# Block 0 of a fused attention and GEGLU block: weight parts issued from another queue, outputs taken out in steps, VectorE in written order

## The chip, the cores and the metric

The kernel runs on one core of a Trainium2 chip. Its time is the device time of one execution in microseconds (us); of several runs the median is given. Engines are named as in the profile: PE (TensorE, matrix products), ACT (ScalarE), DVE (VectorE), POOL (GpSimd) and SP (SyncE, which here only issues DMAs). PSUM is the memory that PE writes into, in banks of 512 floats by 128 partitions; SBUF is the working memory of all engines.

## What is computed

One transformer block in float32 on x of 2048 x 512, with 32 heads of 16 columns that share one key and one value head:

```
q = LN(x) @ wq    k = LN(x) @ wk    v = LN(x) @ wv
p = softmax(q k^T / 4)  per head
h = x + (p v) @ wo
out = h + (gelu(LN(h) @ w_gate) * (LN(h) @ w_up)) @ w_down      # F = 1792
```

## The kernel before, in words

Rows of x are cut into four blocks of 512. A prologue normalizes x, forms the keys and values of all rows and the queries of block 0. Then the attention of blocks 0 to 3 runs, each in eight groups of four heads, and beside it the dense part (`wo`, the gate, up and down products) of the block before; the dense part of block 3 is a tail. float32 products are formed from a high and a low part of each operand, which `split` makes; so `wo` and the FFN weights have to be parted once.

For a group and a chunk of 128 keys, `score` (L614) is called twice. Each call (`scores`, L276) computes two heads' scores, on PE, into a tile `s` of two PSUM banks (three such tiles in block 0), and ACT writes the exponential to `p`. When both calls of a chunk are done, the chunk is put into the list `pend`; `finish` (L593) takes the oldest chunks out and `weigh` (L289) forms the products with the values, 16 matmuls for two chunks, into the one bank `acc`. After 16 chunks `evacuate` (L298) copies `acc` to `oT` on DVE, dumps it to DRAM (`acc_d`), loads it back turned into `oc` (four DMAs), and, after each second group, takes the reciprocal of the row sums in four pieces, multiplies, and splits the result into `o_hi` and `o_lo`.

Block 0 has a loop of its own (L649 to L671), with n counting the score calls: eight groups of 32 calls, and 16 more calls of block 1, up to `lead`. Four calls are called a period here. Beside the scores it carries:

- a step of `work` (the generator `later_q`, L221, over `project_q`, L163) in each period but one of eight: the queries of blocks 1 to 3. Such a step is mostly three matmuls into the single bank `pq`; after each four of them DVE splits the bank, and SP stores the pieces. After the 16 matmul steps of a block come the norms: `pn`, DVE's maximum `q2`, four small POOL operations on `mm` (L201 to L208), and DVE's `m` (L212).
- a step of `parts` (`part_weights`, L328) in most periods: 46 parts, 4 of `wo` and then, for each of 14 FFN columns f, the gate, up and down weights. A step stores the part before (42 stores in all, none for `wo`), loads the next raw weights, and parts the present ones on POOL (two operations, three for the down weights). `w_raw` and `w_both` have two buffers.
- `finish(2)` at a period's end.

PE, ACT and POOL work in the order in which the program is written (`manual_schedule`, L128); in this loop SP does so too (L642), while DVE's instructions are put in order by a scheduler. An engine waits at an instruction until what it needs is there, and everything behind it waits as well. A DMA stands in the queue of the engine that issues it. Semaphore waits between engines are set by the framework.

At n = 256 the rest of the parts is written, the early tiles are released, and the tiles of the dense part take their place; so the first loads of dense tiles (three `w`, L397) wait for the last store of a part. At n = 272 the planned chunks begin (L687), in which dense work is mixed in by written shares; their first dense product is `pp`, which reads `o_hi` and `o_lo` of block 0. `check_bound` (L950) writes a bound of the scores to DRAM and loads it back, and `bound_flag` (L957) makes a flag of it, which decides after everything else whether a second, exact way is taken; it is not taken with these inputs.

Of the kernel before, what the change touches and what calls it, by code (L numbers as in the profile page):

```python
# [9 lines left out]
F32 = mybir.dt.float32  # L10
F32R = mybir.dt.float32r
# [3 lines left out]
ALU = mybir.AluOpType  # L15
# [4 lines left out]
P = 128  # L20
# [16 lines left out]
def kernel(  # L37
# [62 lines left out]
    def split(eng_hi, hi, lo, src, eng_lo=None):  # L100
        if eng_hi is nc.scalar:
            nc.scalar.activation(hi, src, AF.Copy)
        else:
            eng_hi.tensor_copy(hi, src)  # L104
        (eng_lo or nc.vector).tensor_tensor(lo, src, hi.bitcast(F32), op=ALU.subtract)  # L105
# [28 lines left out]
    def run(outer, first):  # L134
# [28 lines left out]
        def project_q(b, eng):  # L163
            tsl = slice(b * T, (b + 1) * T)
            xT_hi, xT_lo = xT[b]
            qss = []
            for c in range(DC):
                pq = psum1(f"pq_{b}_{c}")
                n = 0
                for d in range(DC):  # L170
                    for wt, xt in ((wq_hi, xT_hi), (wq_hi, xT_lo), (wq_lo, xT_hi)):
                        nc.tensor.matmul(  # L172
                            pq, wt[:, d, c * P : (c + 1) * P], xt[:, d, :],
                            start=(n == 0), stop=(n == 3 * DC - 1),
                        )
                        n += 1
                    yield 3
                qh = eb.tile([P, T], F32R, tag="qh", bufs=2, name=f"qh_{b}_{c}")
                ql = eb.tile([P, T], F32R, tag="ql", bufs=2, name=f"ql_{b}_{c}")
                split(eng, qh, ql, pq)  # L180
                qs = eb.tile([P, T], BF16, tag="qs", bufs=DC, name=f"qs_{b}_{c}")
                (nc.vector if b else nc.gpsimd).tensor_tensor(
                    qs, qh.bitcast(F32), qh.bitcast(F32), op=ALU.mult
                )
                qss.append(qs)
                for r0, part in ((0, qh), (DH, ql), (2 * DH, qh)):
                    nc.sync.dma_start(
                        q_d[c * HC : (c + 1) * HC, r0 : r0 + DH, tsl].bitcast(F32),
                        part.bitcast(F32),
                    )  # L190
            yield 3
            pn = psum1(f"pqn_{b}")[:H, :]
            for c in range(DC):
                nc.tensor.matmul(pn, sel[:, c, :], qss[c], start=(c == 0), stop=(c == DC - 1))
            qn = eb.tile([H, T], F32, tag="qn", bufs=1, name=f"qn_{b}")
            nc.vector.tensor_copy(qn, pn)
            nc.vector.tensor_reduce(q2[:, b : b + 1], qn, axis=AX.X, op=ALU.max)
            yield 2

            mm = eb.tile([H, 3], F32, tag="mm", bufs=2, name=f"mm_{b}")  # L200
            nc.gpsimd.tensor_scalar(  # L201
                mm[:, 0:1], q2[:, b : b + 1], k2m, 1e-30, op0=ALU.mult, op1=ALU.add
            )
            nc.gpsimd.tensor_tensor(mm[:, 1:2], mm[:, 0:1], power[:H, 0:1], op=ALU.pow)
            nc.gpsimd.tensor_scalar(
                mm[:, 2:3], mm[:, 0:1], mm[:, 1:2], 0.5, op0=ALU.mult, op1=ALU.mult
            )
            nc.gpsimd.tensor_scalar(  # L208
                mm[:, 1:2], mm[:, 1:2], k2m, 0.5, op0=ALU.mult, op1=ALU.mult
            )  # L210
            m = eb.tile([H, T], F32R, tag="m", bufs=2, name=f"m_{b}")
            nc.vector.tensor_scalar(m, qn, mm[:, 1:2], mm[:, 2:3], op0=ALU.mult, op1=ALU.add)  # L212
            ms[b] = m
            if b > 0:
                nc.sync.dma_start(q_d[:, 3 * DH, tsl].bitcast(F32), m.bitcast(F32))
            yield 2
# [54 lines left out]
            nc.scalar.dma_start(q_d[:, 3 * DH, :T].bitcast(F32), m.bitcast(F32))  # L271
            return qg

        o_blk, pair = {}, [None]

        def scores(i, p, qg, kc, u):  # L276

# [17 lines left out]

        def evacuate(b, g, acc):  # L298
            oT = sb.tile([P, T], F32, tag="oT", bufs=2, name=f"oT_{b}_{g}")
            nc.vector.tensor_copy(oT, acc)  # L300
            nc.sync.dma_start(acc_d[:, g % 4, :], oT)
            c, k = divmod(g, 2)
            if k == 0:
                pair[0] = sb.tile([P, 2, T], F32, tag="oc", bufs=2, name=f"oc_{b}_{c}")
            oc = pair[0]
            view = acc_d[:, g % 4, :].rearrange("(j s e) t -> j e s t", s=2, e=DH)
            for j in range(4):
                r0 = 64 * k + DH * j
                nc.sync.dma_start(oc[r0 : r0 + DH, :, :], view[j])
            if k == 0:  # L310
                return
            if c == 0:
                o_blk[b] = [
                    sb.tile([P, DC, T], F32R, tag=f"o_{w}", bufs=1, name=f"o_{w}_{b}")
                    for w in ("hi", "lo")
                ]
            hi, lo = o_blk[b]

            for t in range(TB):
                sl = slice(t * P, (t + 1) * P)  # L320
                nc.vector.reciprocal(oc[:, 1, sl], oc[:, 1, sl])  # L321
            nc.vector.tensor_tensor(oc[:, 0, :], oc[:, 0, :], oc[:, 1, :], op=ALU.mult)
            split(nc.vector, hi[:, c, :], lo[:, c, :], oc[:, 0, :])

        late = ExitStack()
        db = None
# [1 line left out]
        def part_weights(pw):  # L328
# [4 lines left out]

            def load_wo(c):
                raw = pw.tile([P, D], F32, tag="w_raw", bufs=2, name=f"wo_raw_{c}")
                nc.sync.dma_start(raw, wo_t[:, c, :])
                return raw

            def part_wo(c, raw):
# [1 line left out]

            def load_f(src, name):
                raw = pw.tile([P, D], F32, tag="w_raw", bufs=2, name=f"{name}r")
                nc.sync.dma_start(raw.rearrange("p (c n) -> p c n", n=src.shape[-1]), src)
                return raw

            def part_f(name, halve, raw):
# [4 lines left out]
                return both  # L352

            def store_1(f, k, both):
                nc.sync.dma_start(
                    w1_d[f, :, :, k].bitcast(F32),
                    both.rearrange("p i (c n) -> p i c n", c=DC).bitcast(F32),
                )

            def store_2(f, both):  # L360
                nc.sync.dma_start(w2_d[f].bitcast(F32), both.bitcast(F32))

            steps = [
                (partial(load_wo, c), partial(part_wo, c), None) for c in range(DC)
# [228 lines left out]
        def finish(n):  # L593
            for _ in range(min(n, len(pend))):
                pb, pg, pkc, pp, pacc, _ = pend.pop(0)
                weigh(pacc, pp, pkc)
                if pkc == KC - 1:
                    evacuate(pb, pg, pacc)
# [40 lines left out]

        LEAD = (3, 2, 2)  # L640
        n, lead = 0, 2 * PER + sum(SIZES[: LEAD[0]])
        with tc.manual_schedule(engines={mybir.EngineType.SP}):  # L642
            parts = None
            if first:
                work = later_q()
                parts = part_weights(early.enter_context(tc.tile_pool(name="parts", bufs=1)))


            while n < lead:  # L649
                if n == 2 * PER:  # L650
                    drain()
                    for _ in parts or ():
                        pass
                    parts = None
                    early.close()
                    db = late.enter_context(tc.tile_pool(name="dense", bufs=1))

                if n % 4 == 3 and work is not None and n % (2 * KC) != 11:
                    if next(work, None) is None:
                        work = None  # L660
                score(n)
                n += 1
                if n % 4:
                    continue
                if len(pend) > 2:
                    finish(2)
                if parts is not None and n > 12 and n % 24:
                    next(parts, None)
                if n == 2 * PER + 4:
                    primed = dense(0)  # L670
                    next(primed)  # L671
        if first:
            bound_flag()
        work = primed
        set_banks("ps_rest")
        width = 3
# [10 lines left out]
        for c in range(LEAD[0], (NB - 1) * NG * len(SIZES)):  # L687
# [36 lines left out]
                work = None  # L724
            finish(sum(e[5] < n - 1 for e in pend) if cg < len(SIZES) - 1 else len(pend))
        drain()
        banks.close()
        held_banks.close()
        set_banks("ps_tail")
# [220 lines left out]
    def check_bound(sb, k2m):  # L950
        q2m = sb.tile([H, 1], F32, name="q2m")
        nc.vector.tensor_reduce(q2m, q2, axis=AX.X, op=ALU.max)
        nc.vector.tensor_tensor(q2m, q2m, k2m, op=ALU.mult)
        nc.sync.dma_start(b_d.rearrange("o h -> h o"), q2m)
        nc.sync.dma_start(b2, b_d)

    def bound_flag():  # L957
        nc.vector.tensor_reduce(b1, b2, axis=AX.X, op=ALU.max)

        nc.vector.tensor_scalar(flag, b1, (BOUND_MAX / SCALE) ** 2, None, op0=ALU.is_le)  # L960
# [69 lines left out]
```

## Time and profile before

| | |
|---|---|
| three runs | 1493.0, 1494.29, 1496.1 us; median 1494.29 |
| the profiled execution | 1492.66 us, of which the span of the trace is 1490.9 |
| mean granted PE clock | 0.988 |
| busy in the span | PE 1419.6 us (95%), ACT 1036.6 (70%), DVE 530.4 (36%), POOL 160.9 (11%) |
| DMA | 180.53 MB, 121 GB/s in the mean |

The page cuts the span into 40 slices of 37.3 us and gives each engine's busy share of a slice in tenths. A row of a timeline is: start and duration in us, engine, line, operation, output<-input, shapes, and in brackets how long the engine had been idle before it and who released it. `SPq` and `POOLq` are rows of DMA issues. The granted clock of PE stands in the windows' rows and on the page as a share of full speed.

### The profile page before, as it was taken

How to read it: one execution, taken by the hardware profiler on the slowest of the kernel's cores; microseconds unless marked ns; L12 is line 12 of the kernel's file. 1: busy time of each engine (PE TensorE's matmuls, PEld its weight loads, DVE VectorE, ACT ScalarE, POOL GpSimd, SP SyncE). 2: the span in 40 equal slices, each digit the busy share in tenths (PEclk: the TensorE clock that was granted, in tenths of full speed). 3: DMA queues.
4: the chain of work that ended last, by engine and by line, in shares of the span. 5: the costliest groups of instructions: out<-in, count | busy, mean ns of one | idle time of the engine just before them, and what ended most of it. 6: DMA issues, size and time to landing. Idle time of an engine off the chain costs nothing.

```text
span 1490.9 us, 24774 instructions
## 1 busy us (share of the span) xinstructions
PE 1419.6 (95%) x10412; PEld 755.2 (51%) x10412; DVE 530.4 (36%) x915; ACT 1036.6 (70%) x1139; POOL 160.9 (11%) x211
## 2 busy tenths in 40 slices
PE   6899999979999999999999999999999999997998
PEld 4533333324455555555455555554455555555886
DVE  7311221203342332423342423423342423425665
ACT  6499999977777777777777777777777777760000
POOL 5424445430000000000000000000000000000000
PEclk9899999999999999999999999999999999998999
DMA  4426776664132323222233223232233224232552
GB/s 160 154 72 197 234 222 216 215 202 151 57 111 78 115 82 118 103 85 97 68 111 110 87 79 138 76 121 69 68 111 110 89 76 138 72 106 79 189 193 85
DMA packets 76109, 180.53 MB, mean 121 GB/s; under 512 B 8506, under 2 KB 22842, under 8 KB 68790
## 3 DMA queue, kind: packets, MB, share of 16 engines
q1 hardware_dynamic: 75870, 178.81, 35.9%
q8 instruction: 83, 1.36, 0.4%
q14 instruction: 36, 0.29, 0.1%
q10 hardware_dynamic: 120, 0.07, 0.0%
HBM read 131.13 MB, written 47.71 MB: 120 GB/s over the span
## 4 chain that ended last, share of the span: by engine, by line
PE 64%; ACT 15%; DMA 6%; issue 5%; POOL 5%; DVE 2%; SPq 1%; ACTq 0%; POOLq 0%; DVEq 0%
PE acc L291 26%; ACT p L287 14%; PE s L283 13%; PE pu L412 5%; PE pd L412 4%; PE pg L412 4%; DMA w_1r<-in_B_w_up_dram 3%; PE pg L429 3%; PE pd L429 3%; PE pu L429 3%; DMA acc_d<-oT 2%; PE pp L412 1%; PE pq L172 1%; POOL w_1b L105 1%; PE pp L429 1%
## 5 line engine op out<-in xcount | busy, mean ns | idle before, releaser
L287 ACT ACTIVATE p<-s 128x1024 f32<-128x1024 f32 x1024 | 970.8, 1031 | 282.2 <-PE s L283 281.5
L291 PE MATMUL acc<-p,v_sb 128*32 128x512 f32 x4096 | 493.3, 600 | 4.9 <-DVE oT L300 4.9
L283 PE MATMUL s<-qg,kaug 50*128 50x512 f32 x1984 | 393.2, 434 | 29.9 <-ACT p L287 26.8
L283 PEld LDWEIGHTS s<-qg,kaug 50*128 50x128 f32 x1984 | 172.5, 184 | 311.8 <-ACT p L287 196.4
L291 PEld LDWEIGHTS acc<-p,v_sb 128*32 128x32 f32 x4096 | 112.5, 109 | 253.1 <-issue 237.7
L412 PE MATMUL pg<-x2h,w 64*128 64x512 f32 x672 | 232.0, 391 | 0.8 <-DVE x2h L104 0.8
L412 PE MATMUL pu<-x2h,w 64*128 64x512 f32 x672 | 232.1, 392 | 0.6 <-DVE x2l L105 0.6
L412 PE MATMUL pg<-x2l,w 64*128 64x512 f32 x336 | 131.9, 393 | 0.1
L412 PEld LDWEIGHTS pu<-x2h,w 64*128 64x128 f32 x672 | 124.7, 186 | 14.1 <-issue 1.4
L412 PE MATMUL pu<-x2l,w 64*128 64x512 f32 x336 | 131.6, 392 | 0.0
L412 PEld LDWEIGHTS pg<-x2h,w 64*128 64x128 f32 x672 | 124.7, 186 | 12.3 <-DVE x2h L104 2.0
L113 POOL TENSOR_SCALAR rstd<-mv 128x1 f32<-128x1 f32 x16 | 3.5, 219 | 1025.9 <-DVE mv L111 1025.9
L412 PE MATMUL pd<-w,gh 64*128 64x512 f32 x672 | 105.4, 391 | 0.3 <-DVE mark_pd L420 0.3
L526 ACT ACTIVATE ga<-ga 128x512 f32<-128x512 f32 x56 | 36.2, 646 | 91.4 <-DVE ga L521 91.4
L518 DVE COPY g<-pg 128x512 f32<-128x512 f32 x56 | 38.7, 691 | 143.1 <-PE pg L412 134.9
L554 DVE TENSOR_TENSOR h<-h,pd 128x512 f32<-128x512 f32 x64 | 41.9, 685 | 112.3 <-PE pd L412 91.3
L412 PEld LDWEIGHTS pd<-w,gh 64*128 64x128 f32 x672 | 63.3, 185 | 15.6 <-issue 0.8
L321 DVE RECIPROCAL oc<-oc 128x128 f32<-128x128 f32 x64 | 54.2, 908 | 43.7 <-DMA oc<-acc_d 43.7
L412 PE MATMUL pd<-w,gl 64*128 64x512 f32 x336 | 66.4, 392 | 0.0
L412 PEld LDWEIGHTS pg<-x2l,w 64*128 64x128 f32 x336 | 62.3, 185 | 8.0 <-DVE x2l L105 1.1
L412 PEld LDWEIGHTS pu<-x2l,w 64*128 64x128 f32 x336 | 62.3, 185 | 7.3
L527 DVE SCALAR_TENSOR_TENSOR ga<-ga,g 128x512 f32<-128x512 f32 x56 | 38.8, 692 | 69.8 <-ACT ga L526 69.8
(176 smaller groups left out, 1216.5 us busy)
## 6 DMA issues: line engine op xcount, KB each, us to landing
w<-w_d SPq DMA_DIRECT2D x84, 1024.0 KB
qg<-q_d SPq DMA_DIRECT2D x62, 200.0 KB
q_d<-qh SPq DMA_DIRECT2D x32, 256.0 KB
acc_d<-oT SPq DMA_DIRECT2D x32, 256.0 KB
oc<-acc_d SPq DMA_DIRECT2D x128, 64.0 KB
w_d<-w_0b SPq DMA_DIRECT2D x14, 512.0 KB
w_d<-w_1b SPq DMA_DIRECT2D x14, 512.0 KB
x<-in_A_x_dram SPq DMA_DIRECT2D x16, 256.0 KB
```

The lines of the kernel that those rows point to most:

```text
L105: (eng_lo or nc.vector).tensor_tensor(lo, src, hi.bitcast(F32), op=ALU.subtract)
L172: nc.tensor.matmul(pq, wt[:, d, c * P : (c + 1) * P], xt[:, d, :], start=(n == 0), stop=(n == 3 * DC - 1),)
L283: nc.tensor.matmul(s[:, a, :], kaug[rows, kc * P : (kc + 1) * P], qg[rows, u, :], start=True, stop=True,)
L287: nc.scalar.activation(p[:, 2 * u : 2 * u + 2, :], s, AF.Exp, scale=SCALE)
L291: nc.tensor.matmul(acc[32 * j : 32 * j + 32, :], v_sb[:, kc, :], p[:, j, :], start=(kc == 0), stop=(kc == KC - 1), skip_group_check=True,)
L321: nc.vector.reciprocal(oc[:, 1, sl], oc[:, 1, sl])
L412: nc.tensor.matmul(banks[k], lhsT[rows], rhs[rows], start=(turn == 0 and i == 0), stop=(turn == 1 and i == n - 1), skip_group_check=True,)
L429: nc.tensor.matmul(bank, lhsT, rhs, start=(i == 0), stop=(i == len(ts) - 1))
L518: nc.vector.tensor_copy(g, pg)
L526: nc.scalar.activation(a, a, AF.Tanh, scale=GELU_A * GELU_C)
L527: nc.vector.scalar_tensor_tensor(a, a, 1.0, g, op0=ALU.add, op1=ALU.mult)
L554: nc.vector.tensor_tensor(hs[t], hs[t], pd, op=ALU.add)
```

## The change

- The DMAs of `part_weights` (loads of raw weights and stores of the parts) are issued by GpSimd instead of SP.
- `evacuate` no longer issues everything at once. It makes `oT` and its dump, and puts what follows into a list `outs`: the four loads of `oc` (`turn_out`); after each second group also an empty step, two steps of two reciprocals, and the step `divide`. `take_out` takes one step out in each period. From block 1 on, and at the last group of block 0, all steps are taken at once.
- DVE, too, follows the written order in this loop.
- A step without work (`yield 0`) is put between `mm` and `m`.
- Whether a period gets a step of `work` is settled at its start (`given`; n % 32 is not 8). In a period without one, one chunk is weighed in the middle and one at the end.
- The load of the bound and the flag move behind block 3's attention; the load is issued by GpSimd.

```diff
@@ project_q
             m = eb.tile([H, T], F32R, tag="m", bufs=2, name=f"m_{b}")
+            yield 0
             nc.vector.tensor_scalar(m, qn, mm[:, 1:2], mm[:, 2:3], op0=ALU.mult, op1=ALU.add)
@@ evacuate
+        def take_out():
+            for step in outs.pop(0):
+                step()
...
-            view = acc_d[:, g % 4, :].rearrange("(j s e) t -> j e s t", s=2, e=DH)
-            for j in range(4):
-                r0 = 64 * k + DH * j
-                nc.sync.dma_start(oc[r0 : r0 + DH, :, :], view[j])
-            if k == 0:
-                return
...
+            def turn_out():
+                view = acc_d[:, g % 4, :].rearrange("(j s e) t -> j e s t", s=2, e=DH)
+                for j in range(4):
+                    r0 = 64 * k + DH * j
+                    nc.sync.dma_start(oc[r0 : r0 + DH, :, :], view[j])
...
+            def invert(t):
                 sl = slice(t * P, (t + 1) * P)
                 nc.vector.reciprocal(oc[:, 1, sl], oc[:, 1, sl])
...
+            outs.append([turn_out])
+            if k == 1:
+                outs.append([])
+                outs.extend([partial(invert, t), partial(invert, t + 1)] for t in (0, 2))
+                outs.append([divide])
+
+            if b > 0 or g == NG - 1:
+                while outs:
+                    take_out()
@@ part_weights: load_wo, load_f, store_1, store_2
-                nc.sync.dma_start(raw, wo_t[:, c, :])
+                nc.gpsimd.dma_start(raw, wo_t[:, c, :])
...
-                nc.sync.dma_start(w2_d[f].bitcast(F32), both.bitcast(F32))
+                nc.gpsimd.dma_start(w2_d[f].bitcast(F32), both.bitcast(F32))
@@ run
-        with tc.manual_schedule(engines={mybir.EngineType.SP}):
+        with tc.manual_schedule(engines={mybir.EngineType.SP, mybir.EngineType.DVE}):
...
-                if n % 4 == 3 and work is not None and n % (2 * KC) != 11:
-                    if next(work, None) is None:
-                        work = None
+                if n % 4 == 0:
+                    given = work is not None and n % (2 * KC) != 8
+                if n % 4 == 3 and given and next(work, None) is None:
+                    work = None
                 score(n)
                 n += 1
+                if n % 4 == 2 and not given and len(pend) > 2:
+                    finish(1)
                 if n % 4:
                     continue
                 if len(pend) > 2:
-                    finish(2)
+                    finish(len(pend) - 2)
+                if outs:
+                    take_out()
...
-        if first:
-            bound_flag()
+        assert not outs
...
         drain()
+        if first:
+            bound_flag()
@@ check_bound, bound_flag
-        nc.sync.dma_start(b2, b_d)
...
     def bound_flag():
+        nc.gpsimd.dma_start(b2, b_d)
         nc.vector.tensor_reduce(b1, b2, axis=AX.X, op=ALU.max)
```

More of the change, by code (lines that the diff above doesn't have):

```diff
@@ L272, in first_q @@
             return qg
-        o_blk, pair = {}, [None]
+        o_blk, pair, outs = {}, [None], []
         def scores(i, p, qg, kc, u):
@@ L305, in evacuate, with divide @@
             oc = pair[0]
-            view = acc_d[:, g % 4, :].rearrange("(j s e) t -> j e s t", s=2, e=DH)
-            for j in range(4):
-                r0 = 64 * k + DH * j
-                nc.sync.dma_start(oc[r0 : r0 + DH, :, :], view[j])
-            if k == 0:
-                return
[L312 to L319, printed above, removed]
+            def turn_out():
[4 more added lines that the diff above has]
+            def invert(t):
                 sl = slice(t * P, (t + 1) * P)
                 nc.vector.reciprocal(oc[:, 1, sl], oc[:, 1, sl])
-            nc.vector.tensor_tensor(oc[:, 0, :], oc[:, 0, :], oc[:, 1, :], op=ALU.mult)
-            split(nc.vector, hi[:, c, :], lo[:, c, :], oc[:, 0, :])
+            def divide():
+                if c == 0:
+                    o_blk[b] = [
+                        sb.tile([P, DC, T], F32R, tag=f"o_{w}", bufs=1, name=f"o_{w}_{b}")
+                        for w in ("hi", "lo")
+                    ]
+                hi, lo = o_blk[b]
+                nc.vector.tensor_tensor(oc[:, 0, :], oc[:, 0, :], oc[:, 1, :], op=ALU.mult)
+                split(nc.vector, hi[:, c, :], lo[:, c, :], oc[:, 0, :])
+            outs.append([turn_out])
[6 more added lines that the diff above has]
+                    take_out()
         late = ExitStack()
@@ L343, in load_f @@
                 raw = pw.tile([P, D], F32, tag="w_raw", bufs=2, name=f"{name}r")
-                nc.sync.dma_start(raw.rearrange("p (c n) -> p c n", n=src.shape[-1]), src)
+                nc.gpsimd.dma_start(raw.rearrange("p (c n) -> p c n", n=src.shape[-1]), src)
                 return raw
@@ L354, in store_1 @@
             def store_1(f, k, both):
-                nc.sync.dma_start(
+                nc.gpsimd.dma_start(
                     w1_d[f, :, :, k].bitcast(F32),
```

## The prediction, made before the changed kernel ran

> **What bounds the kernel now.** I read the page first, then ScalarE's timeline over block 0, then the same stretch on all engines where that timeline shows a hole, then SP's and GpSimd's own rows.
>
> ```profile
> span 1490.9 us, 24774 instructions
> PE   6899999979999999999999999999999999997998
> L287 ACT ACTIVATE p<-s 128x1024 f32<-128x1024 f32 x1024 | 970.8, 1031 | 282.2 <-PE s L283 281.5
> POOL rstd L113 <- DVE mv L111: 1025.9, 13, 315.6
> ```
>
> PE is full nearly everywhere except slice 9, about 298 to 335 us; GpSimd has no large work after its weight parts (its longest wait lies behind block 0). So block 0 (66 to 349 us) is the only place where this change can act: the instruction orders of PE and ScalarE from the first dense chunk on are the same in both kernels, and VectorE's differs there only by the two tiny flag operations. The forecast is the change of the moment at which PE reaches the first `pp`.
>
> A period of block 0 is four `score` calls: four exponentials on ScalarE, 16 weighing matmuls and, where a step of projection is given, three more matmuls.
>
> ```profile
> 92.19 3.77 ACT L287 ACTIVATE p<-s 128x1024 f32<-128x1024 f32 x4 [0.33 <-PE s L283]
> 96.27 3.77 ACT L287 ACTIVATE p<-s 128x1024 f32<-128x1024 f32 x4 [0.30 <-PE s L283]
> 299.21 3.77 ACT L287 ACTIVATE p<-s 128x1024 f32<-128x1024 f32 x4 [0.20 <-PE s L283]
> 310.14 3.77 ACT L287 ACTIVATE p<-s 128x1024 f32<-128x1024 f32 x4 [7.16 <-PE s L283]
> 314.10 3.77 ACT L287 ACTIVATE p<-s 128x1024 f32<-128x1024 f32 x4 [0.19 <-PE s L283]
> 291.25 3.77 ACT L287 ACTIVATE p<-s 128x1024 f32<-128x1024 f32 x4 [0.81 <-PE s L283]
> ```
>
> With projection the period is 96.27 - 92.19 = 4.08 us, without it 314.10 - 310.14 = 3.96. One exponential lasts 1.03 and four in a row 3.77, so the next starts 0.913 after the last: 3.67 would be ScalarE's own pace. One hole stands out: 299.21 to 310.14 is 10.93, that is 6.97 over 3.96.
>
> ```profile
> 301.47 1.26 POOL L105 TENSOR_TENSOR w212b<-w212r,w212b 128x512 fp32r<-128x512 f32 x1
> 302.84 0.26 POOL L201 TENSOR_SCALAR mm<-q,k2m 32x1 f32<-32x1 f32 x1
> 304.48 0.53 DVE L212 TENSOR_SCALAR m<-qn,mm 32x512 fp32r<-32x512 f32 x1 [14.22 <-POOL mm L208]
> 304.94 0.67 DVE L300 COPY oT<-acc 128x512 f32<-128x512 f32 x1
> 305.67 3.64 PE L291 MATMUL acc<-p,v_sb 128*32 128x512 f32 x16 [4.89 <-DVE oT L300]
> 311.65 0.64 PE L291 MATMUL acc<-p,v_sb 128*32 128x512 f32 x4
> ```
>
> This is the hole, read upward. PE waits 4.89 for `oT`, since `acc` has one buffer; then its 16 matmuls take 3.64 instead of 1.85 (315.61 below), the clock being lower after the rest. `oT` stood in VectorE's queue behind `m`, which waited 14.22 for GpSimd's `mm`, behind weight part 212.
>
> **The change, part by part.**
>
> (1) *VectorE in program order, and the extra yield.* The seventh `oT` now precedes the last `m`, and `m` comes one given period after its `mm`. The 6.97 go, as does the 0.81 - 0.20 = 0.6 at 291.25 (VectorE then worked through reciprocals and a split that had waited for one transfer). What is late next: the eighth `oT` stands behind that same `m`, eight periods later. I count -7.6.
>
> (2) *Weighing in the middle of a period without projection.* There are 15 such periods: one of eight in each of groups 1 to 7, four in group 8 (n = 232, 244, 248, 252), and four of the lead. PE's work in one is small enough:
>
> ```profile
> 315.18 0.50 PE L283 MATMUL s<-qg,kaug 50*128 50x512 f32 x2 [0.71 <-ACT p L287]
> 315.61 1.92 PE L291 MATMUL acc<-p,v_sb 128*32 128x512 f32 x16
> 317.47 0.96 PE L283 MATMUL s<-qg,kaug 50*128 50x512 f32 x6
> ```
>
> 16 weighing matmuls take 317.47 - 315.61 = 1.86, a pair of scores 0.43 (315.61 - 315.18), four pairs 1.72: 3.58 per period, under ScalarE's 3.67. Now they come in halves of 0.93 while ScalarE still holds up to three finished score tiles, so its gap of 0.19 to 0.30 closes: 15 x (3.96 - 3.69) = -4.0. Bounds: nothing, and 15 x (3.96 - 3.67) = -4.4.
>
> (3) *Outputs in steps.* The reciprocals follow `oT` after two periods (7.4 to 8.2 us). In the row of the last group, whose dump did not queue behind weight transfers, the data were there 344.15 - 337.43 = 6.7 after `oT`; with them it was 281.34 - 266.06 = 15.3.
>
> ```profile
> 266.06 0.69 DVE L300 COPY oT<-acc 128x512 f32<-128x512 f32 x1 [4.37 <-PE acc L291]
> 281.34 3.39 DVE L321 RECIPROCAL oc<-oc 128x128 f32<-128x128 f32 x4 [14.58 <-DMA oc<-acc_d]
> 337.43 0.69 DVE L300 COPY oT<-acc 128x512 f32<-128x512 f32 x1 [21.30 <-PE acc L291]
> 344.15 3.39 DVE L321 RECIPROCAL oc<-oc 128x128 f32<-128x128 f32 x4 [6.03 <-DMA oc<-acc_d]
> 348.76 0.69 DVE L105 TENSOR_TENSOR o_lo<-oc,o_hi 128x512 fp32r<-128x512 f32 x1
> ```
>
> SP's queue holds no weight transfers now, so I take the short case. Twice a split of `pq` (one bank) is queued behind these reciprocals, and PE for the split: up to 1.5 each if the data are 2 late. I also count that `pp` comes nearer to `o_lo`: it is 348.76 + 0.69 = 349.45 now, 12.0 after `oT`, and three faster periods need 12.0 too. Together +1.0.
>
> (4) *The bound's flag.* Two VectorE operations (0.31 us) and a small DMA move behind block 3's attention: nothing, the load being issued long before.
>
> (5) *88 DMAs (46 loads, 42 stores) from SP's queue to GpSimd's.* This decides. GpSimd must now issue them between its own operations, and no row shows what one costs there. The work of one FFN step f is three parts:
>
> ```profile
> 203.02 0.61 POOL L104 CAST w_1b<-w_1r 128x512 fp32r<-128x512 f32 x1 [2.11 <-DMA w_1r<-in_B_w_up_dram]
> 203.71 1.29 POOL L105 TENSOR_TENSOR w_1b<-w_1r,w_1b 128x512 fp32r<-128x512 f32 x1
> 195.47 1.49 POOL L350 TENSOR_SCALAR w25r<-w25r 128x512 f32<-128x512 f32 x1 [5.30 <-DMA w25r<-in_B_w_down_dram]
> 210.70 1.49 POOL L350 TENSOR_SCALAR w26r<-w26r 128x512 f32<-128x512 f32 x1 [5.71 <-DMA w26r<-in_B_w_down_dram]
> 114.42 0.67 DVE L197 TENSOR_REDUCE q<-qn 32x1 f32<-32x512 f32 x1
> 289.23 0.67 DVE L197 TENSOR_REDUCE q<-qn 32x1 f32<-32x512 f32 x1
> ```
>
> 3 x (0.61 + 0.07 + 1.29) + 1.56 = 7.5 us, and 210.70 - 195.47 = 15.2 from one f to the next now: half of it waiting. With d for an issue, f takes 7.5 + 6 d plus about 0.5 of waiting (between a load's issue and its part lie another part and two issues, 1.97 + 2 d at least). In GpSimd's new order the first `mm` stands behind 7 parts, the third behind 45 of the 46: 38 parts, 12.67 f apart. The first cannot come before its `q` (115.1, done 116.4); the third's `q` is two periods later than now, about 296 (289.9 + 8.1, less 2 for faster periods before it). So GpSimd is on time up to (296 - 116.4) / 12.67 = 14.2 per f.
>
> ```profile
> 325.98 0.35 SPq L361 DMA_DIRECT2D w_d<-w213b  x1
> 328.75 1.42 SPq L397 DMA_DIRECT2D w<-w_d  x3
> 338.15 0.34 SPq L301 DMA_DIRECT2D acc_d<-oT  x1
> 340.59 1.73 SPq L309 DMA_DIRECT2D oc<-acc_d  x4
> 325.00:350.00 25.00, 20.71 (x158) 7.01 (x152) 5.89 (x8) 23.65 (x26) 0.95 (x1) 1.00 0.71 263
> ```
>
> There is slack behind it. On SP three `w` loads (3 x 1024 KB, some 12 us at the 263 GB/s of that stretch) wait for the last part, and the dump of the eighth `oT` is queued behind them. The eighth `oT` comes near 327 (337.43 - 7.6 - 12 faster periods). The loads must start by 318; the last store has landed some 9.5 after the third `mm` begins (1.4 for `mm`, 3.5 for the part, two issues, 2.8 for the landing as 328.75 - 325.98 now): `mm` is free until 308.5, or f = 15.2. From there each microsecond delays `o_hi`, and `pp` with it, one for one.
>
> ```profile
> 132.88 0.52 SPq L355 DMA_DIRECT2D w_d<-w_1b  x1
> 133.49 0.56 SPq L344 DMA_DIRECT2D w_0r<-in_B_w_gate_dram  x1
> ```
>
> Bounds for d: 0.52, SP's issue of the same DMA, and 1.49, GpSimd's longest pass over such a tile. I take the middle, 1.0, near neither: f = 7.5 + 6.0 + 0.5 = 14.0, on time, cost nothing. At 0.52 f is 11.1 and it costs nothing either; at 1.49 f is 16.9, the third `mm` at 331, 22 late.
>
> The Trainium skill, page "SBUF — State Buffer", section "SBUF: two separate sides", speaks against this part: a DMA issued from GpSimd needs GpSimd to write its descriptors, and is held off while VectorE runs in a two-port mode (about 620 ns alone, about 3100 beside such a copy). By its 0.62 f would be 11.7, as cheap as at the lower bound.
>
> **Sum.** -7.6 - 4.0 + 1.0 = -10.6. The profiled execution took 1492.66 us (span 1490.9, 1.76 around it), 1.6 under the median of 1494.29; on the median: 1483.7, rounded to **1484**.
>
> **The rivals.**
>
> *A. GpSimd becomes the bound (slower).* Place: the last `m`, and SP's `w` loads ahead of the last dump. Price: 12.67 x (f - 15.2) us; it eats the gain at f = 16.0, that is d = 1.34, and decides from there. At d = 1.49: +22 - 10.6 = +11, 1506. For it: half of the DMAs are in many pieces (the gate and up loads 128 x 4 rows of 512 bytes), and d is unseen. Against: GpSimd waits half of each f today. With d beyond 1.6, 1514 and more. Chance 0.36 for slower; between d = 1.28 and 1.4 it ends within 3 us of before, 0.08.
>
> *B. Weighing one at a time slows the period (slower).* Later in the kernel such chunks exist:
>
> ```profile
> 381.74 1.94 ACT L287 ACTIVATE p<-s 128x1024 f32<-128x1024 f32 x2 [0.35 <-PE s L283]
> 384.34 1.94 ACT L287 ACTIVATE p<-s 128x1024 f32<-128x1024 f32 x2 [0.67 <-PE s L283]
> 382.81 0.14 PEld L291 LDWEIGHTS acc<-p,v_sb 128*32 128x32 f32 x4 [0.80 <-ACT p L287]
> ```
>
> There two exponentials take 2.60, four 5.2: 15 x 1.24 = +18.6, in all 1494.3 - 7.6 + 1 + 18.6 = 1506. Against: there PE weighs the result just made (0.80 waiting for it); here always one two steps old. Chance 0.03.
>
> *C. The change doesn't do what it says:* halves gain nothing and only the hole goes: -6.6, 1488. Chance 0.06.
>
> *D. GpSimd's issues are held off by VectorE.* VectorE has few operations that could do it in block 0: 4 casts of `o_hi` and 3 of `m`; the late ones count. If each held one issue by 2.5 us, 17 us lie on 12.67 f, 1.4 per f: 15.4, cost 2 us, 1486; to turn the sign it must meet many more operations, and then f passes 16 as in A: 1500. This is the skill's rule of above at its own time. Chance 0.03, slower.
>
> **How the numbers follow.** Forecast 0.44, C 0.06: faster 0.50. Within 0.2% (3 us, about what a measurement of this kernel can tell from no change): 0.08. A, B, D: slower 0.42. The range starts at 1480 (-4.4, nothing for (3), and 2 us over) and reaches 1514, where d is 1.6; beyond lie some 0.15. The forecast's own range is 1480 to 1489.
>
> **What would show it.** Right: no hole over 1 us in ScalarE's timeline between 80 and 345; periods without projection at 3.7; GpSimd's third `mm` within a few us of its `q`; SP's `w` loads before 318; `pp` near 339. Wrong: GpSimd's DMA rows over 1.4 us each, VectorE waiting long for `mm`, PE for `oT` or `pq`'s split, and `o_hi` late for `pp`. If the later blocks change their length, the reading that only block 0 matters was wrong.

## The result, and the profile after

The kernel after takes 1497.59 us (median of 18 runs, 1494.78 to 1499.87), the kernel before 1494.72 in the same session (18 runs, 1491.69 to 1496.83): ratio 1.0019, 95% interval [1.0012, 1.0025]. It is 2.9 us slower; 10.6 us faster was forecast. The profiled execution of after took 1497.15 us, 4.5 over that of before.

The page of the kernel after: span, PE's row of the 40 slices, the new DMA queue, and the group of the exponentials.

```profile
span 1495.4 us, 24745 instructions
...
PE   6998999899999999999999999999999999997998
...
q0 software_dynamic: 9760, 34.08, 6.9%
...
L288 ACT ACTIVATE p<-s 128x1024 f32<-128x1024 f32 x1024 | 969.4, 1036 | 287.1 <-PE s L284 286.5
```

The dip to 7 in slice 9 is gone; two slices of 8 stand in its place, slice 4 (112 to 149 us) and slice 8 (262 to 299). The new queue q0 carries the 34 MB that moved to GpSimd. ACT waits 5.0 us longer for `s` than before (286.5 against 281.5).

ScalarE's timeline of the kernel after over block 0, the rows behind its holes and two without one (83.86 and 326.87). The hole at 75.81 is in both kernels (2.57 before):

```profile
75.81 7.44 ACT L288 ACTIVATE p<-s 128x1024 f32<-128x1024 f32 x8 [2.48 <-PE s L284]
83.86 3.77 ACT L288 ACTIVATE p<-s 128x1024 f32<-128x1024 f32 x4 [0.62 <-PE s L284]
...
149.41 1.02 ACT L288 ACTIVATE p<-s 128x1024 f32<-128x1024 f32 x1 [2.27 <-PE s L284]
153.60 3.77 ACT L288 ACTIVATE p<-s 128x1024 f32<-128x1024 f32 x4 [3.16 <-PE s L284]
...
243.78 7.44 ACT L288 ACTIVATE p<-s 128x1024 f32<-128x1024 f32 x8 [1.32 <-PE s L284]
...
287.55 1.02 ACT L288 ACTIVATE p<-s 128x1024 f32<-128x1024 f32 x1 [4.76 <-PE s L284]
290.98 3.77 ACT L288 ACTIVATE p<-s 128x1024 f32<-128x1024 f32 x4 [2.41 <-PE s L284]
...
326.87 27.61 ACT L288 ACTIVATE p<-s 128x1024 f32<-128x1024 f32 x30 [0.20 <-PE s L284]
...
361.29 4.79 ACT L288 ACTIVATE p<-s 128x1024 f32<-128x1024 f32 x5 [2.79 <-PE s L284]
```

The hole of 7.16 at 310.14 is gone. Five new ones, at three places, stand at 149 to 154, 244 and 288 to 291. The last row is the first hole beside dense work, which both kernels have; before, it stood here:

```profile
358.24 4.79 ACT L287 ACTIVATE p<-s 128x1024 f32<-128x1024 f32 x5 [2.79 <-PE s L283]
```

From there on the two keep their distance to within half a microsecond (3.05 here, 3.35 at VectorE's last operation), so block 0 holds the loss; the last 1.15 of the 4.5 lies behind that operation. The eight copies `oT` divide block 0 into groups; their starts, read from VectorE's rows, give its account:

| from `oT` of group | before, us | after, us | difference |
|---|---|---|---|
| 1 to 2 (after: 135.96 to 173.50) | 32.50 | 37.54 | +5.04 |
| 4 to 5 | 32.46 | 33.79 | +1.33 |
| 5 to 6 (the old hole lies here before) | 38.88 | 39.12 | +0.24 |
| 6 to 7 | 32.49 | 29.66 | -2.83 |
| the three others, and the start | | | -0.70 |

The groups are counted from 0. The sum is +3.08. In group 5 to 6 the old hole (38.88 - 32.45 = 6.43) went and a new one of 39.12 - 32.45 = 6.67 came. So 10.0 us were gained and 5.04 + 1.33 + 6.67 = 13.0 lost. The timeline of the kernel after on all engines shows the first of the three places:

```profile
135.96 0.69 DVE L305 COPY oT<-acc 128x512 f32<-128x512 f32 x1 [18.52 <-PE acc L292]
...
143.91 1.76 DVE L321 RECIPROCAL oc<-oc 128x128 f32<-128x128 f32 x2 [7.26 <-DMA oc<-acc_d]
...
145.59 0.63 DVE L104 CAST qh<-pq 128x512 fp32r<-128x512 f32 x1
...
146.25 0.69 DVE L105 TENSOR_TENSOR ql<-pq,qh 128x512 fp32r<-128x512 f32 x1
...
147.00 0.80 PE L172 MATMUL pq<-xT_hi,wq_hi 128*128 128x512 f32 x1 [2.04 <-DVE ql L105]
...
149.31 3.64 PE L292 MATMUL acc<-p,v_sb 128*32 128x512 f32 x16
```

Read it upward. PE's next `pq` waits for the split of the bank (`qh`, `ql`), which needs only `pq`, long finished. VectorE comes to it at 145.59, because two reciprocals stand ahead in its written order, and those wait 7.26 for the transfer of `oc`. PE waits 2.04, and the scores and the 16 weighing matmuls behind `pq` wait with it. These 16 then take 3.64 instead of 1.92. The windows of the kernel after (columns: busy time of PE, PEld, DVE, ACT and POOL with their instructions, then PE's granted clock, DMA share, GB/s) say why:

```profile
136.00:140.50 4.50, 4.50 (x31) 1.69 (x31) 0.65 (x1) 3.92 (x5) 4.14 (x5) 1.00 0.68 229
...
147.00:149.30 2.30, 2.30 (x5) 1.12 (x5) 2.27 (x4) 0.15 (x1) 1.40 (x3) 0.50 0.87 253
149.30:153.00 3.70, 3.70 (x20) 0.72 (x18) 2.81 (x3) 1.02 (x1) 2.37 (x3) 0.50 0.65 193
...
244.00:248.00 4.00, 3.62 (x26) 1.01 (x18) 0.00 (x0) 4.00 (x5) 3.51 (x5) 1.00 0.92 267
```

After the wait of 2.04 us the clock is 0.50 for 6 us; that makes the second ACT hole, 3.16 at 153.60. After the wait of 1.24 at 240 (a split behind `oT`) it stays 1.00, and only one hole follows. Windows of a quarter microsecond put the half clock at about 146.3 to 153.15 here, at 282.9 to 289.65 at the place shown next, and in the kernel before at 303.6 to 310.4: 6.8 us each time (estimated from the means of these windows). It begins during the wait, so after a longer wait less of it is left. The Trainium skill, page "TensorE: Matmul & The Clock Gate", section "Part 1: The HAM clock gate", says that PE falls to half its clock after about 3.4 us of idling; here a wait of 2.04 was enough, with one of 0.41 (up to 144.45) shortly before it.

The other place, between groups 5 and 6, in the same timeline:

```profile
272.45 0.35 SPq L306 DMA_DIRECT2D acc_d<-oT  x1
...
277.89 1.72 SPq L316 DMA_DIRECT2D oc<-acc_d  x4
...
282.04 1.76 DVE L321 RECIPROCAL oc<-oc 128x128 f32<-128x128 f32 x2 [9.61 <-DMA oc<-acc_d]
...
285.13 0.80 PE L172 MATMUL pq<-xT_hi,wq_hi 128*128 128x512 f32 x1 [4.54 <-DVE ql L105]
...
287.43 3.02 PE L292 MATMUL acc<-p,v_sb 128*32 128x512 f32 x16
```

`oT` was copied at 271.73; its dump needed 5.44 us until SP could issue the loads (5.0 of them SP waited for the dump), and the data came 10.3 after `oT`.

### The profile page after: what moved, and what is told of

It reads as the page before. It is cut to its first block, busy times and chain, and to the rows that moved or that the text cites. A ratio compares the mean times of both kernels' runs of the same rounds, so it can differ in the third digit from the quotient of the medians.

```text
span 1495.4 us, 24745 instructions
## 1 busy us (share of the span) xinstructions
PE 1427.1 (95%) x10412; PEld 754.8 (50%) x10412; DVE 531.9 (36%) x915; ACT 1035.3 (69%) x1139; POOL 223.8 (15%) x300
## 4 chain that ended last, share of the span: by engine, by line
PE 74%; ACT 16%; DVE 3%; issue 3%; DMA 2%; SPq 0%; POOL 0%; ACTq 0%; POOLq 0%; DVEq 0%
PE acc L292 30%; PE s L284 16%; ACT p L288 15%; PE pu L430 5%; PE pd L430 4%; PE pg L430 3%; PE pq L172 3%; PE pg L447 3%; PE pu L447 3%; PE pd L447 3%; DMA acc_d<-oT 1%; PE pp L430 1%; DVE oc L321 1%; DMA oc<-acc_d 1%; PE pp L447 1%
## 5 line engine op out<-in xcount | busy, mean ns | idle before, releaser
L288 ACT ACTIVATE p<-s 128x1024 f32<-128x1024 f32 x1024 | 969.4, 1036 | 287.1 <-PE s L284 286.5
L284 PE MATMUL s<-qg,kaug 50*128 50x512 f32 x1984 | 397.5, 436 | 23.1 <-ACT p L288 20.9
```

Of the source, the lines that this page charges most:

```text
L284: nc.tensor.matmul(s[:, a, :], kaug[rows, kc * P : (kc + 1) * P], qg[rows, u, :], start=True, stop=True,)
L288: nc.scalar.activation(p[:, 2 * u : 2 * u + 2, :], s, AF.Exp, scale=SCALE)
```

## The experiments

**Theory H1**: the loss is `pq`'s split standing behind reciprocals that wait for `oc`, with PE's clock on top. **R1**: GpSimd's queue is at fault. **R2**: VectorE's written order as such. **R3**: weighing in mid-period. Ratios are to the kernel before, which was run beside each set on the same chip (medians 1495.84, 1494.61 and 1493.87 for runs 1 to 4, 5 to 8 and 9 to 12). Line numbers are each kernel's own.

### 1. Reciprocals two periods later

```diff
-                outs.append([])
+                outs.extend([] for _ in range(3))
```

> The changed kernel with three empty periods instead of one between the transfer of a pair's second half and its reciprocals, so that the splits of pq at the boundaries of groups 1-2 and 5-6 stand in VectorE's order ahead of the reciprocals that wait for oc. Theory H1 (the loss is pq's split queued behind those reciprocals): the waits of PE's pq for ql of 2.04 us at 147 and 4.54 us at 285 go; the groups of 37.54 and 39.12 us come down to about 32.4, 5 and 6.7 us less: about 1486 us, 11 to 12 under the changed kernel and 8 under the kernel before. Rival R1 (the transfers through acc_d, slowed by GpSimd's queue, hold the work whatever stands behind them): the wait moves with the reciprocals, 1496 to 1499. Rival R2 (VectorE's written order as such): no change, since the order stays written.

Measured: **1485.24 us, ratio 0.9931 [0.9918, 0.9944]**. The timeline of this kernel:

```profile
138.15 0.69 DVE L104 CAST qh<-pq 128x512 fp32r<-128x512 f32 x1 [1.06 <-PE pq L172]
...
143.77 3.39 DVE L321 RECIPROCAL oc<-oc 128x128 f32<-128x128 f32 x4 [3.61 <-DMA oc<-acc_d]
...
145.30 0.51 PE L172 MATMUL pq<-xT_hi,wq_hi 128*128 128x512 f32 x1
...
149.08 3.77 ACT L288 ACTIVATE p<-s 128x1024 f32<-128x1024 f32 x4 [0.61 <-PE s L284]
...
239.29 7.44 ACT L288 ACTIVATE p<-s 128x1024 f32<-128x1024 f32 x8 [1.32 <-PE s L284]
```

The transfer is as slow as before (data 7.4 after `oT` of 136.40), but the split now comes first and PE doesn't wait. Groups 1 to 2 and 5 to 6 take 32.60 and 32.44; the first dense hole stands at 350.12, 11.2 earlier than in after. Only the 1.32 of group 4 to 5 is left. H1 holds, R1 and R2 fall: queue and order are unchanged here.

### 2. Weight transfers back on SP's queue

The first and the last of four such lines (`load_wo`, `load_f`, `store_1`, `store_2`):

```diff
-                nc.gpsimd.dma_start(raw, wo_t[:, c, :])
+                nc.sync.dma_start(raw, wo_t[:, c, :])
...
-                nc.gpsimd.dma_start(w2_d[f].bitcast(F32), both.bitcast(F32))
+                nc.sync.dma_start(w2_d[f].bitcast(F32), both.bitcast(F32))
```

> The changed kernel with its 88 weight transfers back on SP's queue, all else as changed. H1: the transfers through acc_d get behind the weights' again, oT to oc's data grows from 6.4-13.6 us, pq's splits wait as long or longer: 0 to 8 us slower than the changed kernel, 1497 to 1505. R1 (GpSimd's queue is at fault): the waits shrink and the time falls to 1488-1492.

Measured: 1500.23 us, 1.0024 [1.0012, 1.0037]. The interval overlaps that of after, so the time alone decides little. The timeline:

```profile
147.51 1.76 DVE L321 RECIPROCAL oc<-oc 128x128 f32<-128x128 f32 x2 [10.21 <-DMA oc<-acc_d]
...
150.60 0.79 PE L172 MATMUL pq<-xT_hi,wq_hi 128*128 128x512 f32 x1 [5.02 <-DVE ql L105]
```

The same wait, longer (5.02 for 2.04), as H1 says; at this place nothing shrank, against R1. Here the move of the weights did help: in this run SP stood 6.4 us at the store of a part that GpSimd had not finished, the dump behind it left 2.7 us after `oT` was done (139.98 for 137.30), and the data came 10.9 after `oT` instead of 7.95. Between groups 5 and 6 the data came 9.9 after `oT` (274.22 to 284.16), on GpSimd's queue 10.3: there the transfer was slow on either queue. The Trainium skill, page "DMA: Bandwidth & Descriptors", section "Issuing engines are not separate DMA queues", says this: all DMAs interleave on the same 16 engines, whoever issues them, so that only issue time is saved. The place between groups 5 and 6 agrees (from the dump to its loads 4.93 us here, 5.44 with the weights on GpSimd's queue). The place between 1 and 2 does not: there the move saved SP a wait for GpSimd's part, not issue time.

### 3. VectorE's order left to the scheduler

```diff
-        with tc.manual_schedule(engines={mybir.EngineType.SP, mybir.EngineType.DVE}):
+        with tc.manual_schedule(engines={mybir.EngineType.SP}):
```

> The changed kernel with VectorE's order left to the scheduler, which puts pq's splits of the boundaries 1-2 and 5-6 ahead of the pairs' reciprocals. H1: the same gain as with three empty periods, less what m ahead of oT of group 6 may cost: 1486 to 1489. R1: no change, 1496 to 1499. R2: 1486 to 1490, as H1; this run and the one with later reciprocals tell H1 (both faster) from R2 (only this one).

Measured: 1499.54 us, 1.0029 [1.0016, 1.0041]; the number I expected was wrong. The profile is of the slowest of its 11 runs (1503.35). The waits for `ql` went (groups 1 to 2 and 4 to 5 take 32.63 and 32.49), but group 5 to 6 takes 50.64:

```profile
315.82 0.53 DVE L213 TENSOR_SCALAR m<-qn,mm 32x512 fp32r<-32x512 f32 x1 [18.30 <-POOL mm L208]
...
316.29 0.67 DVE L305 COPY oT<-acc 128x512 f32<-128x512 f32 x1
...
321.19 7.44 ACT L288 ACTIVATE p<-s 128x1024 f32<-128x1024 f32 x8 [18.87 <-PE s L284]
```

The scheduler put `m` ahead of the seventh `oT`, as in the kernel before, and GpSimd is later with `mm`. That hole, 7.16 before, is 18.87 here, more than the split's waits had cost. So once GpSimd issues the DMAs, the yield alone doesn't remove the old hole; it takes the written order, too.

### 4. No weighing in mid-period

```diff
-                if n % 4 == 2 and not given and len(pend) > 2:
-                    finish(1)
```

> The changed kernel without the weighing of one batch in mid-period where no projection is given (its two batches are weighed at the period's end, as before the change). H1: the last group's 29.66 us go back to about 32.5, the rest stays: 2.8 us slower, about 1500.5. Rival R3 (weighing in mid-period is at fault): faster than the changed kernel, 1494 or less, with the long groups shorter.

Measured: 1498.22 us, 1.0015 [1.0005, 1.0026]. All five holes are still there, so R3 falls. 2.8 us were expected; the price of the step isn't told apart from nothing by these times, but the last group takes 31.72 us in the profile instead of 29.66. Run 8 prices it without the holes.

### 5. The kernel before with the yield alone

```diff
             m = eb.tile([H, T], F32R, tag="m", bufs=2, name=f"m_{b}")
+            yield 0
```

> The kernel before with the extra yield ahead of m and nothing else: weights on SP's queue, outputs taken out at once, VectorE's order left to the scheduler, which now puts the copy oT of group 6 ahead of the third m and both splits of pq ahead of the reciprocals. By step 1 of the prediction the hole of 6.97 us goes and nothing takes its place: 7 us faster than before, about 1488. The rival here: the hole was only where another wait showed, and m or the transfers are late next: within 2 us of before.

Measured: 1490.78 us, 0.9974 [0.9959, 0.9988]: faster by 3.8 (12 runs, 1485.19 to 1492.34). The profiled run is the fastest of them, and there the hole is gone and nothing came in its place (first dense hole at 350.96, 7.3 earlier):

```profile
298.14 0.69 DVE L300 COPY oT<-acc 128x512 f32<-128x512 f32 x1 [0.20 <-PE acc L291]
...
310.96 0.26 POOL L201 TENSOR_SCALAR mm<-q,k2m 32x1 f32<-32x1 f32 x1
```

`mm` comes 13 us after `oT`, and nobody on the path waits for it. The mechanism of step 1 is shown in this trace; what the ten runs between 1489 and 1493 spent the rest on was not recorded.

### 6. No empty period: the opposite dose

```diff
             if k == 1:
-                outs.append([])
```

> The changed kernel with no empty period instead of one, the opposite dose of the first run: all four reciprocals now stand ahead of pq's split at the boundaries 1-2 and 5-6. H1 (the split queued behind the reciprocals): each of the two splits comes two reciprocals later, 1.76 us each time beside the wait for oc, so 3.5 to 5 us slower than the changed kernel, 1501 to 1503. If something else made the loss, for instance GpSimd's queue, the number of empty periods changes nothing: 1496 to 1499.

Measured: 1500.61 us, 1.0038 [1.0026, 1.0051], 3.0 over after, a little less than the 3.5 to 5 expected. The timeline:

```profile
280.93 3.39 DVE L321 RECIPROCAL oc<-oc 128x128 f32<-128x128 f32 x4 [9.13 <-DMA oc<-acc_d]
...
285.64 0.79 PE L172 MATMUL pq<-xT_hi,wq_hi 128*128 128x512 f32 x1 [5.67 <-DVE ql L105]
...
288.06 1.03 ACT L288 ACTIVATE p<-s 128x1024 f32<-128x1024 f32 x1 [5.89 <-PE s L284]
```

Four reciprocals stand ahead of the split and PE waits 5.67 instead of 4.54. The number of empty periods moves the time in both directions: 1500.6 with none, 1497.6 with one, 1485.2 with three (ratios 1.0038, 1.0019, 0.9931).

### 7. The kernel before with the weights on GpSimd's queue

The first of the same four lines:

```diff
-                nc.sync.dma_start(raw, wo_t[:, c, :])
+                nc.gpsimd.dma_start(raw, wo_t[:, c, :])
```

> The kernel before with only the weight transfers on GpSimd's queue; VectorE's order is the scheduler's and keeps the third m ahead of group 6's copy oT. By step 5 the issues cost GpSimd some 0.65 us each and nobody waits for its parts: but the step of parts that stands ahead of mm gets longer by 4 issues and their waits, 4 to 5 us, and the hole at 299 with it: 1496 to 1503. R1 (the queue itself disturbs the transfers through acc_d): more holes elsewhere, 1505 and up. If the queue cost nothing anywhere: 1494.

Measured: 1495.84 us, 1.0005 [0.9988, 1.0022]: no difference. The hole of `m` ahead of `oT` moved; the timeline has it one projection earlier:

```profile
205.88 0.79 DVE L212 TENSOR_SCALAR m<-qn,mm 32x512 fp32r<-32x512 f32 x1 [6.48 <-POOL mm L208]
...
211.17 3.77 ACT L287 ACTIVATE p<-s 128x1024 f32<-128x1024 f32 x4 [6.61 <-PE s L283]
```

A second hole, 3.40 at 311.50, stands where the old one stood, with another cause: VectorE waits 9.33 us there for the load of the bound (up to 307.06), `oT` stands behind the flag, and PE waits 2.17 for `oT`. In the time, the queue alone neither wins nor loses.

### 8. Run 1 without weighing in mid-period

The edits of runs 1 and 4 together.

> The first run (three empty periods) without the weighing in mid-period: prices that step where no other hole moves. From the last group's 29.66 us against 32.49: 2.8 us slower than the first run, about 1488; step 2 of the prediction said 4.0, so 1489; if weighing in mid-period gives nothing, 1485.

Measured: 1487.49 us, 0.9949 [0.9930, 0.9969], 2.25 over run 1. From the first `oT` to the first dense hole it takes 351.07 - 102.90 = 248.17, run 1 350.12 - 104.19 = 245.93: 2.24 in the profile, too. Step 2 is worth about 2.2 us here, not 4.0. (The ratios differ by 2.7 us, but their intervals overlap.)

### 9. Splits of `pq` a period earlier

The kernel after; the second added line stands behind the split and its stores:

```diff
                         n += 1
-                    yield 3
+                    if b == 0 or d < DC - 1: yield 3
...
+                if b: yield 3
```

> The changed kernel with its one empty period, but each split of pq written right behind the chunk's last matmuls, a period earlier, for the second, third and fourth projection. The reciprocals stay where they are; the splits of the boundaries 1-2, 4-5 and 5-6 now stand ahead of them and of oT. H1: the waits of PE's pq for ql go as with three empty periods, and the 1.32 us hole at the boundary 4-5 with them: 12 to 13 us under the changed kernel, about 1485. If the place of the reciprocals (their wait, the transfers) cost by itself: 1490 to 1498.

Measured: **1483.45 us, 0.9934 [0.9915, 0.9954]**, the lowest median of all. The timeline:

```profile
137.69 0.69 DVE L104 CAST qh<-pq 128x512 fp32r<-128x512 f32 x1 [1.05 <-PE pq L172]
...
143.96 3.39 DVE L321 RECIPROCAL oc<-oc 128x128 f32<-128x128 f32 x4 [4.16 <-DMA oc<-acc_d]
...
267.25 0.69 DVE L104 CAST qh<-pq 128x512 fp32r<-128x512 f32 x1 [1.07 <-PE pq L172]
```

Here the reciprocals wait where they waited in after, with one empty period; only the split went in front. All three places are mended, the 1.32 of group 4 to 5 included (32.50). So the place of the reciprocals costs nothing by itself: it is what stands behind them.

### 10. Both cures

The edits of runs 1 and 9 together.

> Both cures: splits a period earlier and three empty periods. H1: nothing of the two big waits is left to gain, so only the 1.32 us hole at the boundary 4-5 goes beside the first run: about 1484. If the two cures added up, it would be 1475.

Measured: 1483.96 us, 0.9937 [0.9918, 0.9956]. The two cures don't add up: they remove the same wait.

### 11. Run 1 with the weights on SP's queue

The edits of runs 1 and 2 together.

> The first run (three empty periods) with the weight transfers back on SP's queue: prices the queue where the splits are out of the reciprocals' way. If GpSimd's queue gives nothing on this path: within 2 us of the first run, 1484 to 1487. If the transfers through acc_d, slower behind the weights', still reach a waiting split or q's loads: 1488 to 1493, with new waits of PE for qg or oc's data.

Measured: 1488.82 us, 0.9972 [0.9955, 0.9988] (12 runs, 1484.19 to 1494.90). By the ratios GpSimd's queue gives 6 us here, by the medians 3.6. The timeline shows where:

```profile
328.77 0.33 SPq L306 DMA_DIRECT2D acc_d<-oT  x1
...
336.94 1.74 SPq L316 DMA_DIRECT2D oc<-acc_d  x4
...
340.50 3.39 DVE L321 RECIPROCAL oc<-oc 128x128 f32<-128x128 f32 x4 [11.76 <-DMA oc<-acc_d]
...
352.41 4.79 ACT L288 ACTIVATE p<-s 128x1024 f32<-128x1024 f32 x5 [4.18 <-PE s L284]
```

The last dump of block 0 takes 8.17 us (4.75 in run 1), `o_lo` ends at 345.80, and PE, already in `pp`, waits: ACT has new holes of 2.12 at 346.29 and 4.18 at 352.41. The second of the two cases expected came true, by the late data of `oc` and not by `qg`. Why the dump is slower here was not tried; the three `w` loads were issued 4.1 us ahead of it, in run 1 7.0.

### 12. The kernel before with the yield and the written order

The edit of run 5, and DVE in the set of `manual_schedule` as in the change.

> The kernel before with VectorE in written order and the extra yield, outputs still taken out at once and weights on SP's queue. All four reciprocals of a pair then stand right behind oT, ahead of every split that follows. H1: the waits of the zero-empty run at the boundaries 1-2 and 5-6, and longer, since the data come behind the weights: 1498 to 1506. If the written order costs nothing without the steps: about 1488, like the run with the yield alone.

Measured: 1506.95 us, 1.0092 [1.0071, 1.0113]: 16 us over the yield alone, a little more than expected. The timeline:

```profile
286.08 3.39 DVE L321 RECIPROCAL oc<-oc 128x128 f32<-128x128 f32 x4 [9.41 <-DMA oc<-acc_d]
...
294.00 0.79 PE L172 MATMUL pq<-xT_hi,wq_hi 128*128 128x512 f32 x1 [9.14 <-DVE ql L105]
...
296.41 1.03 ACT L287 ACTIVATE p<-s 128x1024 f32<-128x1024 f32 x1 [9.06 <-PE s L283]
```

With the outputs taken out at once, the reciprocals, the product and the split into `o_hi` and `o_lo` all stand ahead of `pq`'s split. Run 2 has the same order and the same queue, but takes the outputs out in steps; it stands 6.7 under this run, of which the weighing in mid-period explains some 2 (the flag's place differs, too). So the steps are what makes the written order bearable, and one empty period is too few.

## Why the prediction was wrong, point by point

- **What bounds it** (block 0 alone can move the time): right. Of +4.5 in the spans +3.05 stand at the first dense hole; 0.3 came between there and VectorE's last operation and 1.15 behind it, and neither was explained.
- **(1) Order and yield, -7.6**: right in mechanism and about in size: the old hole had lengthened its group by 6.43 and the next by 0.78 (32.49, but 31.71 in run 5, which has neither the hole nor weighing in mid-period), and the yield alone moves the profile by 7.3. On the median of 12 runs it is worth 3.8.
- **(2) Weighing in mid-period, -4.0**: too large; measured 2.24 (run 8) and 2.06 (the last group, 29.66, takes 31.72 in runs 4 and 8). The -2.83 of the table is not this step alone: 0.78 of it belongs to the old hole. 30 exponentials in 27.61 us are 0.92 each, 3.68 a period, as I said (four times the 0.913 I read is 3.65, not 3.67, which changes little); but this holds only where such periods follow each other. A single one gains nothing: from 75.81 to 83.86 there are 8.05 us for two periods, before 84.03 - 75.95 = 8.08, since the row behind it waits 0.62. I multiplied 15 periods where about 8 counted.
- **(3) Outputs in steps, +1.0: this step failed.** It named the right mechanism ("Twice a split of `pq` (one bank) is queued behind these reciprocals, and PE for the split: up to 1.5 each if the data are 2 late") and mis-sized it: the two splits cost 5.04 and 6.67, 11.7 us together. A third split, which stands behind `oT` alone, cost 1.33 that no term had: 13.0 in all. Runs 1, 6 and 9 show that it is this queue. Three things were wrong. The short case of 6.7 us was taken because SP's queue held no weights any more; the data came 7.95, 13.55 and 10.31 us after the second `oT` of the first three pairs and 6.37 only after the last, and the move had made only the first of them faster (run 2: 10.90, 11.20 and 9.94). I took a wait only, and not what follows it: PE's slower clock was in the quoted rows (3.64 for 1.85 after the old hole), and what followed added 3.0 us to the wait of 2.04 (5.04 in all) and 2.1 to that of 4.54 (6.67). Nearly all of it is the clock: the 16 products took 3.64 and 3.02 instead of 1.92, the five matmuls ahead of them 2.3 instead of 1.3. And I had VectorE's new order at hand, from which run 1's cure could be read. The rest of the term, `pp` close behind `o_lo`, cost nothing: `o_lo` ended at 352.17, and the first `pp` began at 353.0 without a wait (three faster periods are 11.1 by my own 3.69, not 12.0).
- **(4) The flag, 0**: nothing in the kernel after speaks against it; it was not tried by itself. Run 7 shows that the old place can cost: there the flag's wait stands ahead of `oT`, and its group is 3.3 longer (35.73). In the kernel before VectorE waited as long (10.17, up to 315.78) and nobody behind it.
- **(5) 88 DMAs on GpSimd's queue, 0**: right for this kernel, and it held most of my chance for slower. Groups of GpSimd's DMA rows in the kernel after (line, output<-input, count, busy us, mean ns):

```profile
L362 POOL DMA_DIRECT2D w_0r<-in_B_w_gate_dram x14 | 11.9, 847 | 0.3 <-POOL wo_lo L105 0.3
...
L373 POOL DMA_DIRECT2D w_d<-w_0b x14 | 9.8, 698 | 4.2 <-POOL w_0b L105 4.2
...
L354 POOL DMA_DIRECT2D wo_raw<-in_A_wo_dram x4 | 2.4, 611 | 0.6 <-POOL wo_lo L105 0.6
```

  An issue costs 0.61 to 0.85 us, below the 1.0 taken and far from the 1.34 at which rival A decides. The third `mm` began 0.1 after its `q` (310.03 for 309.24 + 0.67). That is partly luck: f was 15.3 (from `w21r` at 125.21 to `w212r` at 293.87, 11 f), not 14.0, since GpSimd waited longer for its loads than the 0.5 I took (17.8 us for `w_1r` alone), and `q` came at 309.9 instead of 296. In run 9 `q` is there at 297.0 and `mm` comes at 310.2, later than the 308.5 I allowed; no wait of PE for `pp` followed, so there was more slack than I counted. SP's `w` loads came at 322.67 instead of before 318, 12.6 after `mm` began, where I took 9.5. The 3.1 us that the prediction cites from the Trainium skill's page "SBUF — State Buffer" was not seen in GpSimd's issues: none in the timeline is longer than 0.86. The page's two times are those of a whole DMA, which I set against an issue.
- **The rivals**: none of A to D shows in the traces (by A's own formula the end within 3 us is d = 1.30 to 1.38, not 1.28 to 1.4). The slower end came from the term in (3) that I had priced at one. The list of signs was right: PE waiting for "`pq`'s split" is the one that stood there.

The forecast of 1484 is close to what the change gives when step 3 is mended: 1483.45 and 1485.24. That is partly luck: step 2 then gives 1.8 less than forecast, and the 1.0 of step 3, which isn't paid, and 0.7 that no term had nearly make up for it.

## What to carry to other kernels

When an engine is put into written order, list for each instruction that waits on a transfer what stands behind it and who waits for that; then place what needs only finished data (here the split) ahead, or the waiting one later. A step that is hidden by one period has to be sized by the slowest transfer in the trace, not the fastest, and a wait of PE by the wait plus the slower clock behind it. A second cure of the same wait adds nothing.

## What the runs showed that was not expected

- PE's granted clock fell to 0.50 in a wait of 2.04 us, about 1.4 us after PE's last matmul, and stayed there for 6.8, as it did after the waits of 4.54 here and 4.89 in the kernel before; in a wait of 1.24 it did not fall.
- The spread of the runs differed, not only the median: with the splits in front and the weights on GpSimd's queue the kernels ranged over 1.7 to 3.2 us (5 or 6 runs each), with the weights on SP's over 7.2 (run 5) and 10.7 (run 11; 12 runs each; more runs spread wider by themselves). Which transfers make that spread was not recorded.
